# Chunk attention and a leaky-ReLU MLP in one Trainium2 kernel: weights of one more group turned by TensorE, and another order on SyncE's queue

## The chip, the cores and the metric

The kernel runs on one core of one Trainium2 chip. The metric is the device time of the program on that core in microseconds (us); given times are medians of several runs. All inputs are float32 in device memory, and the result is written there in float32.

## The reference

Attention runs inside chunks of 64 tokens only (batch 8, 8 heads, 576 tokens, head size 64); its result, with the heads side by side, is the input of an MLP of 4608 tokens, 512 wide with 2048 hidden units.

```python
q_c = q.reshape(B, H, nc, chunk, D)          # chunk = 64, nc = 9; k_c and v_c alike
scores = scale * np.matmul(q_c, k_c.transpose(0, 1, 2, 4, 3))
scores = scores - np.max(scores, axis=-1, keepdims=True)
attn = np.exp(scores)
attn = attn / (np.sum(attn, axis=-1, keepdims=True) + 1e-09)
out = np.matmul(attn, v_c)
...
x = np.ascontiguousarray(attn_out.transpose(0, 2, 1, 3)).reshape(B * S, H * D)
h = x @ w_in
g = np.maximum(0.01 * h, h)
return g @ w_out
```

## The kernel before

**Attention by groups.** The 4608 tokens are 36 groups of 128 tokens, each two chunks of 64, all 8 heads. For a group u:

- GpSimd issues the loads of q and k (line 79), which convert to float16; each has 8 buffers.
- q and k are transposed: groups 0 to 9 on TensorE (lines 388 and 393), with a copy out of the bank behind it; from group 10 on by a DMA that SyncE issues (line 409 for q into QT, line 412 for k into KT, 4 buffers each). This is called a *turn* of q or k. GpSimd copies QT into QZ (line 418).
- TensorE makes the scores Sp (line 425). VectorE takes the maximum (435) and subtracts it (439), ScalarE takes the exponential (445), VectorE sums it and inverts the sum (451 to 455), and GpSimd, VectorE for some groups, multiplies the two into the attention weights en (461).
- The weights are transposed into et, which has 4 buffers. For groups 0 to 7, and for those listed in BY_PE (line 42), this is done by four transposes on TensorE (469) and a copy on ScalarE (100) or VectorE (102), called e and d2. For the rest it is a DMA on SyncE's queue (480), called d.
- TensorE multiplies them with the values (491, into xp), and ScalarE copies xp to xT, the input of the MLP (504).

**The MLP by blocks.** Four blocks of 128 tokens (0 to 3) come first, and then eight of 512 (4 to 11). The first layer is plain for blocks 0 to 5 (169, with ScalarE's leaky ReLU at 180); from block 6 on it is a fast product in the manner of Strassen and Winograd (307), with sums on VectorE (216, 219) and copies on ScalarE (183). The second layer is plain for blocks 0 to 3 (194), and fast from block 4 on (355): VectorE forms sums S of pieces of gT (216, 219), TensorE multiplies, and ScalarE and VectorE (219) write the results into osb, which has 3 buffers. SyncE stores osb (line 213 for plain blocks, 367 for fast ones). A fast block has two halves, and each half two sides, so that it is stored in several pieces.

**What sets the order.** Nothing is scheduled while the program is built. It makes a list of steps, such as "scores of group 22" or "turn of k of group 22", and run() emits them in the order of the list ORDER (line 643 on). An entry holds the number of the step, a fill, and the bank of TensorE's accumulator memory or the buffer that the step takes. Each engine's instructions stand in the order in which they are emitted, and each engine works through its own queue in that order: an instruction that waits holds up all that stands behind it on its engine. SyncE's queue holds the turns and the stores together; GpSimd's holds the loads, the copies into QZ and the multiplications of line 461. ON (line 615) names the engine of the steps that have a choice.

A fill such as (39, 7) means that ahead of the step TensorE multiplies ones into bank 7, 39 units of 128 columns (line 510); nobody reads the result. All fills stand in the first 34 us.

```python
def stage_c(u, e):                  # "d2": bank -> et, engine e
def stage_d(u):                     # "d": en -> et by SyncE's DMA
if u < UE or u in BY_PE:            # e and d2, else d
```

Of the kernel before, what the change touches and what calls it, by code (L numbers as in the profile page):

```python
# [16 lines left out]
def kernel(  # L17
# [24 lines left out]
    BY_PE = [8, 9, 18]  # L42
# [567 lines left out]
    def arrive_v(b, c0, c1, after=(), **kw):  # L610
# [6 lines left out]
        ('zv', 0, 2): 'dve', ('zq', 2): 'dve', ('zv', 1, 2): 'act', ('zv', 1, 3): 'act', ('p', 0, 0): 'dve', ('p', 0, 1): 'dve', ('p', 1, 1): 'act',  # L617
        ('p', 1, 0): 'dve', ('zq', 3): 'pool', ('n', 0): 'dve', ('p', 2, 0): 'act', ('p', 2, 1): 'act', ('d2', 0): 'dve', ('v_p', 0, 0): 'act', ('n', 1): 'dve',
        ('v_p', 1, 1): 'act', ('v_p', 2, 1): 'act', ('v_p', 3, 0): 'pool', ('v_p', 0, 1): 'act', ('v_p', 1, 0): 'dve', ('v_p', 3, 1): 'pool',
        ('v_p', 4, 0): 'act', ('v_p', 5, 1): 'act', ('v_p', 2, 0): 'pool', ('d2', 1): 'dve', ('v_p', 4, 1): 'dve', ('v_p', 5, 0): 'dve', ('p', 3, 0): 'dve',  # L620
        ('p', 3, 1): 'dve', ('zv', 2, 1): 'pool', ('n', 2): 'dve', ('d2', 2): 'act', ('zv', 2, 0): 'pool', ('zv', 3, 1): 'act', ('zv', 2, 2): 'pool',
        ('zv', 3, 3): 'act', ('zv', 2, 3): 'pool', ('v_p', 7, 1): 'dve', ('v_p', 6, 1): 'act', ('v_p', 6, 0): 'act', ('p', 4, 1): 'act', ('p', 4, 0): 'dve',
        ('n', 3): 'dve', ('d2', 3): 'dve', ('zv', 3, 2): 'act', ('p', 5, 0): 'act', ('p', 5, 1): 'act', ('v_p', 7, 0): 'pool', ('zv', 3, 0): 'act',
        ('p', 6, 0): 'dve', ('p', 6, 1): 'dve', ('v_p', 8, 0): 'dve', ('v_p', 8, 1): 'dve', ('n', 4): 'dve', ('p', 7, 1): 'dve', ('p', 7, 0): 'dve',
# [525 lines left out]
```

## Time and profile before

| what | value |
|---|---|
| median of 3 runs | 276.37 us (275.36, 276.37, 276.54) |
| profiled execution | 278.43 us |
| its span (first to last instruction on the engines) | 276.7 us |
| granted TensorE clock over the span | 1.0 |
| DMA traffic | 38.64 MB, mean 140 GB/s |

The profile is of one execution. A row of the timeline holds the start, the busy time, the engine, the source line, the operation with its output and its inputs, the shapes, and the number of instructions in the row; in brackets stands the idle time of the engine ahead of the row and what ended it. A row of the list of waits holds the engine and the operation that waited, what released it, the sum, the count and the longest. Rows without a start hold a DMA and its time from issue to landing. SPq and POOLq are the queues of DMAs that SyncE and GpSimd issue: there a row's time is that of the issue. The rows themselves stand with the steps of the prediction that use them.

GpSimd's loads (line 79) and SyncE's turns and stores use the same 16 DMA engines. By slices of 6.9 us, these are busy over 90% from the start to 173 us, as row DMA of the page shows (tenths of busy time):

```profile
DMA  9999999999999999999999999999953050040016
```

### The profile page before, as it was taken

The page shows a single profiled execution, that of the slowest core. Times are in us where ns is not written, and L with a number is a line of the kernel's source. Part 1 is how long each engine was busy: PE and PEld are TensorE (multiplying, and loading weights), DVE is VectorE, ACT ScalarE, POOL GpSimd, SP SyncE. Part 2 cuts the span into 40 slices and gives each one's busy share as a digit, 9 for nine tenths or more (in the row PEclk, how much of TensorE's full clock was granted, in tenths as well). Part 3 has the DMA queues.
Part 4 walks back from the last instruction along what each step waited for, and adds up shares of the span by engine and source line. Part 5 has one row for each costly group of instructions (what it writes and reads, how often), then busy time and mean ns, then how long its engine had stood idle before and what let it go on. Part 6 is the DMA issues. An engine that isn't in the chain of part 4 may idle for free.

```text
span 276.7 us, 7688 instructions
## 1 busy us (share of the span) xinstructions
PE 266.4 (96%) x3116; PEld 231.0 (84%) x3116; DVE 209.7 (76%) x376; ACT 196.5 (71%) x370; POOL 159.7 (58%) x199
## 2 busy tenths in 40 slices
PE   7999999999998999999799999999999999999995
PEld 3568678789897899999699898979999899888884
DVE  5896286869888798899788997868998873825462
ACT  6488955767764835899698549889687897467821
POOL 8999784695996996928927798635653020000000
PEclk9999999999999999999999999999999999999999
DMA  9999999999999999999999999999953050040016
GB/s 135 156 191 185 181 173 176 141 167 209 121 117 153 169 179 163 169 168 191 124 136 189 130 167 183 143 173 143 220 140 40 2 178 14 0 154 0 28 51 229
DMA packets 163635, 38.64 MB, mean 140 GB/s; under 512 B 154640, under 2 KB 159248, under 8 KB 163600
## 3 DMA queue, kind: packets, MB, share of 16 engines
q0 software_dynamic: 114384, 18.09, 101.3%
q1 hardware_dynamic: 48176, 19.80, 41.6%
q8 instruction: 24, 0.39, 0.6%
q10 hardware_dynamic: 1040, 0.26, 0.4%
q14 instruction: 11, 0.09, 0.1%
HBM read 36.70 MB, written 9.44 MB: 167 GB/s over the span
## 4 chain that ended last, share of the span: by engine, by line
PE 74%; DMA 10%; POOL 7%; DVE 4%; issue 2%; ACT 2%; POOLq 0%; DVEq 0%
PE oA L355 17%; PE hA L307 14%; PE hT L169 9%; PE oC L355 9%; PE hC L307 7%; PE oP L194 5%; DMA et<-en 5%; PE oB L355 4%; PE hB L307 4%; DMA KT<-k_in 3%; DMA q_in<-in_q_dram 3%; PE xp L491 2%; PE Sp L425 2%; POOL q_in L79 2%; POOL en L461 2%
## 5 line engine op out<-in xcount | busy, mean ns | idle before, releaser
L355 PEld LDWEIGHTS <-gT 128*128 128x128 f16 x640 | 61.3, 98 | 6.7
L461 POOL TENSOR_TENSOR en<-ex,zi 128x512 f16<-128x512 f16 x23 | 26.5, 1152 | 47.3 <-DVE zi L455 17.6
L219 DVE TENSOR_TENSOR tmp<-hC,tmp 128x512 f32<-128x512 f32 x48 | 32.1, 683 | 19.9 <-PE hC L307 18.1
L169 PE MATMUL hT<-xT,w_inT 128*128 128x128 f16 (+1 forms) x512 | 46.0, 246 | 1.0 <-ACT xT L504 0.9
L169 PEld LDWEIGHTS <-w_inT 128*128 128x128 f16 x512 | 39.4, 98 | 4.8 <-issue 1.3
L307 PEld LDWEIGHTS <-VF 128*128 128x128 f16 x512 | 39.4, 98 | 2.8
L418 POOL COPY QZ<-QT 64x512 f16<-64x512 f16 x52 | 34.8, 669 | 4.0 <-DMA QT<-q_in 1.8
L79 POOL DMA_DIRECT2D q_in<-in_q_dram x39 | 33.6, 864 | 4.6 <-DMA w_outT<-in_moe_w_out_dram 2.5
L79 POOL DMA_DIRECT2D k_in<-in_k_dram x39 | 33.5, 861 | 2.2 <-DVE gT L216 1.1
L183 ACT ACTIVATE tmp<-hA 128x512 f32<-128x512 f32 x48 | 27.7, 598 | 8.9 <-PE hA L307 8.3
L180 ACT ACTIVATE gT<-hT 128x512 f16<-128x512 f32 x48 | 26.6, 599 | 8.9 <-PE hT L169 8.8
L355 PE MATMUL oA<-WF,gT 128*128 128x256 f16 x256 | 32.5, 273 | 0.0
L307 PEld LDWEIGHTS <-w_inT 128*128 128x128 f16 x384 | 30.2, 98 | 2.2
L435 DVE TENSOR_REDUCE mx<-Sp 128x8 f32<-128x512 f32 x36 | 24.5, 682 | 8.4 <-PE Sp L425 8.3
L180 ACT ACTIVATE gT<-tmp 128x512 f16<-128x512 f32 x48 | 29.6, 629 | 1.4 <-DVE tmp L219 1.2
L445 ACT ACTIVATE ex<-sh 128x512 f16<-128x512 f32 x36 | 22.7, 630 | 10.3 <-DVE sh L439 9.3
L451 DVE TENSOR_REDUCE z<-ex 128x8 f32<-128x512 f16 x36 | 24.4, 677 | 5.8 <-ACT ex L445 5.7
L504 ACT ACTIVATE xT<-xp 128x512 f16<-128x512 f32 x36 | 21.2, 599 | 10.1 <-PE xp L491 10.0
L307 PE MATMUL hA<-XF,VF 128*128 128x128 f16 (+1 forms) x256 | 27.5, 246 | 0.0
L355 PEld LDWEIGHTS <-S 128*128 128x128 f16 x256 | 24.5, 98 | 2.7
L439 DVE TENSOR_TENSOR sh<-Sp,mx 128x512 f32<-128x512 f32 x36 | 24.4, 683 | 0.5
L183 ACT ACTIVATE hB<-hA 128x512 f32<-128x512 f32 x24 | 13.9, 588 | 12.1 <-PE hA L307 11.9
(77 smaller groups left out, 493.6 us busy)
## 6 DMA issues: line engine op xcount, KB each, us to landing
out_dram<-osb SPq DMA_DIRECT2D x14, 512.0 KB, 3.8
VB<-in_v_dram POOLq DMA_DIRECT2D x14, 288.0 KB, 7.9
q_in<-in_q_dram POOLq DMA_DIRECT2D x31, 128.0 KB, 7.2
k_in<-in_k_dram POOLq DMA_DIRECT2D x31, 128.0 KB, 6.8
w_inT<-in_moe_w_in_dram POOLq DMA_DIRECT2D x8, 256.0 KB, 7.6
w_outT<-in_moe_w_out_dram POOLq DMA_DIRECT2D x4, 512.0 KB, 9.4
out_dram<-osb SPq DMA_DIRECT2D x6, 256.0 KB, 4.2
v_t<-in_v_dram POOLq DMA_DIRECT2D x4, 128.0 KB, 7.2
```

The lines of the kernel that those rows point to most:

```text
L79: nc.gpsimd.dma_start(out=t[a - u * G:z - u * G], in_=src[b, :, r:r + z - a, :].rearrange("h p d -> p h d"))
L169: nc.tensor.matmul(out=hT[:, i, :], lhsT=w_inT[:, t, fc * 128:(fc + 1) * 128], rhs=xT[:, t, r0 % RING:r0 % RING + tb], start=(i == 0 and t ...
L180: nc.scalar.activation(out=to, in_=of, func=AFT.Prelu, bias=0.0, scale=1.0, alpha=0.01)
L183: nc.scalar.activation(out=to, in_=of, func=AFT.Copy, bias=0.0, scale=1.0)
L219: (nc.vector if e == "dve" else nc.gpsimd).tensor_tensor(out=to, in0=a, in1=b, op=ALU.add)
L307: nc.tensor.matmul(out=PA[key][:, c, :], lhsT=w[:, t, fc * 128:(fc + 1) * 128], rhs=x[:, t, :], start=(m in (1, 5) and c == 0 and t == 0), ...
L355: nc.tensor.matmul(out=to, lhsT=lhs[:, fc, p * 128:(p + 1) * 128], rhs=rhs[:, fc, :], start=(fresh and fc == 0), stop=(fc == HB - 1), skip ...
L418: nc.gpsimd.tensor_copy(out=QZ[u % NQZ][part, :, :, s, :], in_=QT[u][part].rearrange("p i (e t) -> p i e t", e=2))
L435: nc.vector.tensor_reduce(out=MX[u], in_=SP[u], axis=AXL.X, op=ALU.max)
L439: nc.vector.tensor_tensor(out=SH[u], in0=SP.pop(u), in1=MX.pop(u).unsqueeze(2).to_broadcast((128, 8, CH)), op=ALU.subtract)
L451: nc.vector.tensor_reduce(out=z, in_=E[u], axis=AXL.X, op=ALU.add)
L461: eng.tensor_tensor(out=E[u], in0=ex, in1=ZI.pop(u).unsqueeze(2).to_broadcast((128, 8, CH)), op=ALU.mult)
```

## The change

Group 11 is added to BY_PE. Its weights are transposed on TensorE, and copied by VectorE, where SyncE's DMA did it. The list has one step more by this (e and d2 in place of d), so that the numbers in ORDER behind it shift by one, and both tables are written anew.

```diff
-    BY_PE = [8, 9, 18]
+    BY_PE = [8, 9, 11, 18]
...
     ON = {
...
+        ('vf', 1): 'dve', ('n', 11): 'pool', ('d2', 11): 'dve', ('vf', 2): 'dve', ('n', 12): 'pool', ('sf', 4, 2): 'dve', ('n', 13): 'pool', ('vf', 3): 'dve',
...
     ORDER = [
...
-        (115, (9, 1), 3), (113, 0), (88, 0, 4), (13, 0), (116, 0), (89, 0), (144, (5, 1), 5), (117, 0, 6), (18, 0), (145, 0), (90, 0), (118, 0), (23, 0),
```

What the two tables hold differs in these places only:

- **Fills.** The steps keep their places, the numbers change. Ahead of the transposes of q and k of groups 1 to 3, as before: 39, 14, 9, 5 and 67 units, together 134; now 39, 0, 9, 19 and 90, together 157. Around the scores and weights of groups 1 and 2, before 16, 6, 13, 4 and 2 units; now 19, 0, 17 and 4, with 3 ahead of a first-layer block.
- **TensorE.** The second first-layer block of block 1 stands ahead of the transposes of group 2's weights (469), and the values product of group 2 (491) behind a block more. Group 9's weights are transposed one step earlier, ahead of the values product of group 8, and its own values product comes three steps earlier, ahead of the scores of group 11 and a second-layer block. Group 11's transposes stand behind the scores of group 13, and its values product comes one block earlier.
- **ScalarE.** Two copies move, both of group 9. **VectorE.** One copy is added, et of group 11. **GpSimd.** The order is the same.
- **SyncE.** From group 10 on the turns and the stores stand in another order. The last two stores are exchanged.

Banks and buffers have other numbers in many entries; what they hold is the same.

On ScalarE, around 71 us (the evictions gT<-hT are those of block 4's first layer, the two copies et<-tpe and xT<-xp that are moved are those of group 9):

```order
 L100 ACTIVATE et<-tpe 128x512
-L180 ACTIVATE gT<-hT 128x2x256 x4
-L504 ACTIVATE xT<-xp 128x4x128
-L183 ACTIVATE tmp<-oA 128x512
-L100 ACTIVATE et<-tpe 128x512
-L504 ACTIVATE xT<-xp 128x4x128
+L180 ACTIVATE gT<-hT 128x2x256 x3
+L100 ACTIVATE et<-tpe 128x512
+L180 ACTIVATE gT<-hT 128x2x256
+L504 ACTIVATE xT<-xp 128x4x128 x2
+L183 ACTIVATE tmp<-oA 128x512
```

The copy of group 9's weights has moved ahead of an eviction, and its xT ahead of an eviction of an output block.

On SyncE, from the turn of group 17's weights on (some 117 to 135 us). Before, the rows are: weights of group 17, k of 21, store of block 4, q of 22, q of 23, weights of 19, store of block 5's first part, k of 22, weights of 20.

```order
L480 DMA_TRANSPOSE et_2287<-en_2274 128x4x128
L412 DMA_TRANSPOSE KT_2312<-k_in_1877 128x4x128
L367 DMA out_0_dram<-osb_1927 128x2x512
L409 DMA_TRANSPOSE QT_2359<-q_in_1924 128x4x128
L409 DMA_TRANSPOSE QT_2390<-q_in_1819 128x4x128
L480 DMA_TRANSPOSE et_2465<-en_2437 128x4x128
L367 DMA out_0_dram<-osb_2001 128x2x512
L412 DMA_TRANSPOSE KT_2538<-k_in_1976 128x4x128
L480 DMA_TRANSPOSE et_2585<-en_2560 128x4x128
```

Of the change: weights of group 17, q of 22, store of block 4, k of 22, store of block 5's second part, q of 23, weights of 19, weights of 20.

```order
L480 DMA_TRANSPOSE et_2297<-en_2284 128x4x128
L409 DMA_TRANSPOSE QT_2322<-q_in_1900 128x4x128
L367 DMA out_0_dram<-osb_1934 128x2x512
L412 DMA_TRANSPOSE KT_2369<-k_in_1959 128x4x128
L367 DMA out_0_dram<-osb_2333 128x2x512
L409 DMA_TRANSPOSE QT_2420<-q_in_1808 128x4x128
L480 DMA_TRANSPOSE et_2476<-en_2448 128x4x128
L480 DMA_TRANSPOSE et_2593<-en_2568 128x4x128
```

The turn of k of group 22 now stands ahead of group 19's weights, with the store of block 5's second part behind it, which was issued near 148 us before; the store of the first part is gone from here. That one now comes ten rows further on, behind turns of groups 23 to 26 and the weights of group 21:

```order
L412 DMA_TRANSPOSE KT_2621<-k_in_1686 128x4x128
L412 DMA_TRANSPOSE KT_2660<-k_in_2257 128x4x128
L409 DMA_TRANSPOSE QT_2695<-q_in_2501 128x4x128
L409 DMA_TRANSPOSE QT_2744<-q_in_2233 128x4x128
L412 DMA_TRANSPOSE KT_2873<-k_in_2716 128x4x128
L409 DMA_TRANSPOSE QT_2910<-q_in_2623 128x4x128
L480 DMA_TRANSPOSE et_2939<-en_2852 128x4x128
L367 DMA out_0_dram<-osb_1997 128x2x512
```

The fifth row is the turn of k of group 25, which waits for its load, and the last the store of the first part.

On SyncE, some 174 to 190 us. Before: weights of groups 27 and 28, k of 31, store of a part of block 6, k of 32, weights of 29, q of 32.

```order
L480 DMA_TRANSPOSE et_3606<-en_3580 128x4x128
L480 DMA_TRANSPOSE et_3646<-en_3624 128x4x128
L412 DMA_TRANSPOSE KT_3675<-k_in_3285 128x4x128
L367 DMA out_0_dram<-osb_3113 128x2x512
L412 DMA_TRANSPOSE KT_3709<-k_in_3537 128x4x128
L480 DMA_TRANSPOSE et_3735<-en_3713 128x4x128
L409 DMA_TRANSPOSE QT_3764<-q_in_3270 128x4x128
```

Of the change: the store of the part of block 6, k of 31, weights of 27, q of 32, k of 32, weights of 28, k of 33, weights of 29.

```order
L367 DMA out_0_dram<-osb_3123 128x2x512
L412 DMA_TRANSPOSE KT_3546<-k_in_3296 128x4x128
L480 DMA_TRANSPOSE et_3618<-en_3591 128x4x128
L409 DMA_TRANSPOSE QT_3634<-q_in_3280 128x4x128
L412 DMA_TRANSPOSE KT_3660<-k_in_3532 128x4x128
L480 DMA_TRANSPOSE et_3689<-en_3637 128x4x128
L412 DMA_TRANSPOSE KT_3721<-k_in_3476 128x4x128
L480 DMA_TRANSPOSE et_3747<-en_3725 128x4x128
```

The weights of group 28 have moved behind the turn of k of group 32, and those of 29 behind that of 33.

More of the change, by code (lines that the diff above doesn't have):

```diff
@@ L616 @@
         ('zq', 0): 'dve', ('zq', 1): 'dve', ('zv', 0, 3): 'dve', ('zv', 0, 0): 'dve', ('zv', 1, 1): 'act', ('zv', 0, 1): 'dve', ('zv', 1, 0): 'act',
-        ('zv', 0, 2): 'dve', ('zq', 2): 'dve', ('zv', 1, 2): 'act', ('zv', 1, 3): 'act', ('p', 0, 0): 'dve', ('p', 0, 1): 'dve', ('p', 1, 1): 'act',
-        ('p', 1, 0): 'dve', ('zq', 3): 'pool', ('n', 0): 'dve', ('p', 2, 0): 'act', ('p', 2, 1): 'act', ('d2', 0): 'dve', ('v_p', 0, 0): 'act', ('n', 1): 'dve',
-        ('v_p', 1, 1): 'act', ('v_p', 2, 1): 'act', ('v_p', 3, 0): 'pool', ('v_p', 0, 1): 'act', ('v_p', 1, 0): 'dve', ('v_p', 3, 1): 'pool',
@@ L620 @@
[L620 to L623, printed above, removed]
+        ('zv', 0, 2): 'dve', ('zq', 2): 'dve', ('zv', 1, 2): 'act', ('zv', 1, 3): 'act', ('p', 0, 0): 'dve', ('p', 1, 1): 'act', ('p', 0, 1): 'dve',
@@ new lines @@
+        ('p', 1, 0): 'dve', ('zq', 3): 'pool', ('n', 0): 'dve', ('p', 2, 0): 'act', ('d2', 0): 'dve', ('n', 1): 'dve', ('p', 2, 1): 'act', ('v_p', 0, 0): 'act',
+        ('v_p', 1, 1): 'act', ('v_p', 2, 1): 'act', ('v_p', 3, 0): 'pool', ('v_p', 1, 0): 'dve', ('v_p', 0, 1): 'act', ('v_p', 3, 1): 'pool',
+        ('v_p', 4, 0): 'act', ('v_p', 2, 0): 'pool', ('d2', 1): 'dve', ('v_p', 5, 1): 'act', ('v_p', 4, 1): 'dve', ('v_p', 5, 0): 'dve', ('p', 3, 0): 'dve',
+        ('p', 3, 1): 'dve', ('zv', 2, 1): 'pool', ('n', 2): 'dve', ('zv', 2, 0): 'pool', ('zv', 2, 2): 'pool', ('d2', 2): 'act', ('zv', 2, 3): 'pool',
@@ L624 @@
+        ('zv', 3, 1): 'act', ('zv', 3, 3): 'act', ('v_p', 7, 1): 'dve', ('v_p', 6, 1): 'act', ('v_p', 6, 0): 'act', ('p', 4, 0): 'dve', ('n', 3): 'dve',
+        ('p', 4, 1): 'act', ('d2', 3): 'dve', ('v_p', 7, 0): 'pool', ('zv', 3, 2): 'act', ('p', 5, 0): 'act', ('p', 5, 1): 'act', ('zv', 3, 0): 'act',
         ('p', 6, 0): 'dve', ('p', 6, 1): 'dve', ('v_p', 8, 0): 'dve', ('v_p', 8, 1): 'dve', ('n', 4): 'dve', ('p', 7, 1): 'dve', ('p', 7, 0): 'dve',
         ('d2', 4): 'act', ('n', 5): 'dve', ('d2', 5): 'dve', ('wf', 0): 'dve', ('p', 8, 1): 'act', ('wf', 1): 'dve', ('p', 9, 1): 'act', ('wf', 2): 'dve',
[16 rows of a table removed]
[16 rows of a table added]
```

236 rows, old and new, of tables (ON, ORDER) are left out of this document.

## The prediction, made before the changed kernel ran

> **What bounds the kernel now.** I read the page, then TensorE's rows in the list of waits, then the timeline around each wait, then the chain.
>
> ```profile
> PE 266.4 (96%) x3116; PEld 231.0 (84%) x3116; DVE 209.7 (76%) x376; ACT 196.5 (71%) x370; POOL 159.7 (58%) x199
> PE Sp L425 <- DMA KT<-k_in: 2.0, 1, 2.0
> PE hT L169 <- ACT xT L504: 0.9, 2, 0.7
> PE xp L491 <- DMA et<-en: 0.9, 2, 0.5
> ```
>
> TensorE is idle for some 10 us of 276.7. What it waits for, apart from the start, are single late inputs. In order of time:
>
> ```profile
> 9.73 3.78 PE L510 MATMUL idle<-XF 128*128 128x512 f16 x17
> 13.76 0.62 PE L388 MATMUL qp<-ident,q_in 128*128 128x128 f16 x8 [0.25 <-DMA q_in<-in_q_dram]
> 22.56 0.40 PE L469 MATMUL tpe<-ident,en 128*128 128x128 f16 x4 [0.50 <-DVE en L461]
> 74.95 0.81 PE L169 MATMUL hT<-xT,w_inT 128*128 128x256 f16 x6 [0.69 <-ACT xT L504]
> 88.55 0.39 PE L491 MATMUL xp<-et,VB 128*128 128x64 f16 x8 [0.51 <-DMA et<-en]
> 89.62 0.60 PE L169 MATMUL hT<-xT,w_inT 128*128 128x256 f16 x4 [0.22 <-ACT xT L504]
> 134.90 0.39 PE L425 MATMUL Sp<-KT,QZ 128*128 128x64 f16 x8 [1.99 <-DMA KT<-k_in]
> 185.07 0.39 PE L491 MATMUL xp<-et,VB 128*128 128x64 f16 x8 [0.39 <-DMA et<-en]
> ```
>
> The reader is to see the wait in the brackets; each also costs some 0.15 us, because the weight load behind it starts late. But TensorE does not lead everywhere: the chain runs over GpSimd from 67 to 81 us, with hardly a gap, and TensorE catches up with it.
>
> ```profile
> 67.00 1.04 POOL en L461
> 80.27 1.03 POOL en L461
> ```
>
> The profiled execution took 278.43 us, 1.7 more than its span and 2.1 more than the median of 276.37. The sum below is a difference, made on its rows and put on the median.
>
> **The front: more fill.** Ahead of the transposes of q of group 3 (13.76) the fill grows from 14+9+5+67 = 95 to 9+19+90 = 118 units of 128 columns. The 67 units took 3.78 us, 0.056 each, so 23 more are 1.3 us. Their cover is the 0.25 us for which TensorE waited for q, so these transposes come about 1.0 late. Everything up to the weights of group 2 hangs on them, and the transposes of those weights, at 22.56, now also stand behind one more first-layer block; they start about 1.1 later. What they release is ScalarE's queue:
>
> ```profile
> 22.99 0.60 ACT L100 ACTIVATE et<-tpe 128x512 f16<-128x512 f16 x1 [0.29 <-PE tpe L469]
> 33.91 0.60 ACT L504 ACTIVATE xT<-xp 128x512 f16<-128x512 f32 x1
> 34.72 1.06 PE L169 MATMUL hT<-xT,w_inT 128*128 128x128 f16 x16
> ```
>
> Between the first two rows ScalarE has no wait of 0.15 us, so its delay arrives whole at xT of group 3, which TensorE reads at 34.72 at once. The waits at 22.56 and 24 go away on TensorE, and come back as waits for ScalarE. **+1.1** (ends +0.2, if the q loads land a microsecond later than here and hide the fill, and +1.3).
>
> **The moves at 71 and 88.** Group 9's transposes, its values product and, on ScalarE, its two copies come earlier: the product passes a score step and an output block of 0.87, together 1.1 us, more than the wait at 74.95. **-0.8.** Group 11's weights no longer go through SP: the waits at 88.55 and 89.62 go, 0.73 with some 0.3 of weight loads, for four transposes of 0.23. The added copy of 0.4 on VectorE lies beside TensorE's blocks; without that cover it would cost its 0.4. **-0.8.**
>
> **GpSimd stays late.** It follows the scores of groups 8 and 9, which follow the front, so it keeps the front's +1.1 while TensorE has won 1.6.
>
> ```profile
> 92.49 1.06 POOL L461 TENSOR_TENSOR en<-ex,zi 128x512 f16<-128x512 f16 x1
> 93.58 0.63 ACT L445 ACTIVATE ex<-sh 128x512 f16<-128x512 f32 x1
> 94.60 2.05 ACT L180 ACTIVATE gT<-hT 128x512 f16<-128x512 f32 x4
> ```
>
> ScalarE's exp at 93.58 starts as GpSimd's multiply ends (93.55), and the evictions queue behind it. The first, done at 95.2, frees a bank for a block that TensorE began at 95.73. It is now done at 96.3, TensorE is there at 95.2. **+1.0** (ends 0, if the front costs nothing, and 1.2). Up to here +0.5.
>
> **SP between 117 and 150.** This is the core of the change.
>
> ```profile
> 120.22 0.65 SPq L367 DMA_DIRECT2D out_dram<-osb  x1
> 121.01 3.34 SPq L409 DMA_TRANSPOSE QT<-q_in  x2
> 124.88 1.19 SPq L480 DMA_TRANSPOSE et<-en  x1
> 126.52 0.38 SPq L367 DMA_DIRECT2D out_dram<-osb  x1
> 127.07 2.20 SPq L412 DMA_TRANSPOSE KT<-k_in  x1
> ```
>
> The turn of k of group 22 (127.07) stood behind the store of block 5; now it issues some 4 us sooner. The wait at 134.90 goes with its weight load: **-2.1**. But the weights of group 19 (124.88) are now behind that turn and the other store, less one turn: about 1.6 later, 126.5. There they meet loads:
>
> ```profile
> 126.31 0.88 POOL L79 DMA_DIRECT2D k_in<-in_k_dram  x1
> et<-en SPq DMA_TRANSPOSE x1, 2.6
> out_dram<-osb SPq DMA_DIRECT2D x1, 512.0 KB, 6.4
> KT<-k_in SPq DMA_TRANSPOSE x1, 7.7
> 131.62 0.40 PE L491 MATMUL xp<-et,VB 128*128 128x64 f16 x8
> ```
>
> The three middle rows are the landing times of what SP issued at 124.88, 126.52 and 127.07: 2.6 before the load, 6.4 and 7.7 after it. Group 19 is needed at 131.62, now 132.1. It lands between 129.1 (2.6) and 134.2 (7.7); with 6.4, the nearest, at 132.9. **+1.2** with the weight load (ends 0 and 2.3). [...]
>
> The store of block 5 goes the other way, behind the turn of k of group 25, whose input loads late:
>
> ```profile
> k_in<-in_k_dram POOLq DMA_DIRECT2D x1, 128.0 KB, 10.0
> out_dram<-osb SPq DMA_DIRECT2D x1, 512.0 KB, 3.6
> 152.99 0.68 DVE L219 TENSOR_TENSOR osb<-oC,tmp 128x512 f32<-128x512 f32 x1
> 157.29 1.22 DVE L216 TENSOR_TENSOR S<-S,gT 128x2048 f16<-128x2048 f16 x1
> 159.69 0.49 PE L355 MATMUL oA<-WF,S 128*128 128x256 f16 x3
> ```
>
> The load was issued at 133.2 and took 10.0; with +0.5 it lands at 143.7. Three turns of 1.3 follow, so the store issues at 147.6 instead of 126.5. It lands at 151.2 by the store issued at 148.45 (3.6), or 154.0 by its own 6.4. VectorE's sum at 152.99 writes the buffer that it frees, and is due at 152.6 less what has been won; behind it in VectorE's queue is S, which ends at 158.5 with 1.2 us of slack to 159.69. If group 19 cost nothing, the sum is due at 151.4, waits 2.6, and TensorE loses 1.4; else 0 to 0.4. **+0.3** (ends 0 and 1.4).
>
> **SP between 174 and 190.** The weights of groups 28 and 29 now stand behind turns of k:
>
> ```profile
> k_in<-in_k_dram POOLq DMA_DIRECT2D x1, 128.0 KB, 9.0
> 183.91 1.50 SPq L412 DMA_TRANSPOSE KT<-k_in  x1
> et<-en SPq DMA_TRANSPOSE x1, 4.8
> 192.52 0.40 PE L491 MATMUL xp<-et,VB 128*128 128x64 f16 x8
> ```
>
> The load at 174.7 lands at 183.7. Group 32's turn takes 1.3, group 28's 1.3, another turn of k 1.5 (183.91), and group 29 issues at 187.8; with the 4.8 of group 28 before (180.6) it lands at 192.6, against 192.52 less what was won. **+0.6** (ends 0 and 1.2). The wait at 185.07 follows GpSimd and stays. The stores at the end are swapped in pairs that wait for the same blocks: 0.
>
> **Sum:** 1.1 - 0.8 - 0.8 + 1.0 - 2.1 + 1.2 + 0.3 + 0.6 = +0.5: 278.9 for a profiled execution, 276.9 for the median.
>
> **The rivals.** (a) *The queue holds*: landings stay below some 5.5 us, groups 19 and 29 and the store are in time, and only front and GpSimd cost: 1.1 - 1.6 + 1.0 - 2.1 = -1.6, **274.8**. For it speaks that 2.6 and 3.6 occur in the same stretches. Against: the 6.4 and 7.7 beside them. (b) *The wait changes place*, and grows: group 19 lands as the turn of 127.07 did, 7.7 after its issue. It decides from about 5.6 us and takes back more than the 2.1 at 7.7. Then 2.3 for group 19, 0.5 for the store, 1.2 for 28 and 29: 0.5 - 2.1 + 4.0 = +2.4, **278.8**. For it: GpSimd's loads surround this place in both kernels. Against: SP may be held less than I reckon, and then the turn slips in ahead of the load.
>
> **How the numbers follow.** A measurement of this kernel can tell about 0.5% (1.4 us) from no change. The forecast, +0.5, has 0.42; (a) has 0.24; (b) has 0.34, since two of its three pieces need only one late load each. The range reaches to both rivals with little beyond, 274.6 to 279.4; the forecast's own is 275.0 to 277.7. Hence faster 0.24, same 0.42, slower 0.34.
>
> **What would show it.** Right: q of group 3 transposed near 14.8 and no wait for a q load there; no wait at group 9, 11 and 22's places; a new wait for ScalarE near 35 and 96; group 19's values product, or the block behind S near 159, waiting. Wrong: the long fill ends in a wait for q again (the front costs nothing); GpSimd's multiply near 92 not later than before; group 19's turn landing in 3 us; or a new wait of over a microsecond at a place not named here.

## The result and the profile after

| | before | changed |
|---|---|---|
| median | 275.93 us (275.36 to 276.54, 4 runs) | 279.68 us (278.21 to 283.01, 4 runs) |
| ratio | 1 | 1.0119, 95% interval 1.0087 to 1.0151 |
| profiled execution, its span | 278.43, 276.7 | 283.01, 281.2 |

The changed kernel is slower by 1.2%, some 3.3 us. Medians here count all executions, and ratios leave out those that are over 1.5% above the fastest of their kernel, among them the profiled one of the changed kernel, so that a ratio says less than the medians (here 1.36%) where a kernel's executions lie far apart.

TensorE's rows of the list of waits of the changed kernel (sum in us, count, longest; the row of the start, its second, is left out):

```profile
PE xp L491 <- DMA k_in<-in_k_dram: 2.9, 1, 2.9
...
PE xp L491 <- ACT ex L445: 1.3, 1, 1.3
PE kp L393 <- DMA k_in<-in_k_dram: 1.1, 1, 1.1
PE hT L169 <- ACT xT L504: 1.0, 2, 0.6
PE xp L491 <- DMA et<-en: 0.3, 1, 0.3
```

The waits of before for KT (group 22) and for group 11's weights are gone, as forecast, and so is the one for q in the front. In their place stand a wait of 1.15 us for k in the front, one of 1.28 near 84 at group 10's values product, and one of 2.93:

```profile
84.61 0.41 PE L491 MATMUL xp<-et,VB 128*128 128x64 f16 x8 [1.28 <-ACT ex L445]
```

TensorE's timeline around the longest:

```profile
187.00 0.39 PE L491 MATMUL xp<-et,VB 128*128 128x64 f16 x8 [2.93 <-DMA k_in<-in_k_dram]
187.23 1.04 PE L355 MATMUL oA<-w_outT,gT 128*128 128x256 f16 x8
188.10 1.76 PE L307 MATMUL hA<-xT,w_inT 128*128 128x256 f16 x8
189.66 2.89 PE L355 MATMUL oB<-w_outT,gT 128*128 128x256 f16 x16
192.38 1.04 PE L307 MATMUL hA<-XF,VF 128*128 128x256 f16 x8
...
194.15 0.39 PE L491 MATMUL xp<-et,VB 128*128 128x64 f16 x8 [0.29 <-DMA et<-en]
```

The row at 187.00 is the values product of group 27, the one at 194.15 that of group 28. Behind the wait the rows are slow: eight matmuls of 256 columns take 1.76 us at 188.10 and 1.04 at 192.38. The table by stretches shows why (start and end, length, busy time and count of TensorE, then the granted clock, the DMA share and GB/s):

```profile
186.00:188.00 2.00, 1.00 (x16) 1.00 0.96 75
188.00:190.00 2.00, 2.00 (x13) 0.56 1.94 138
190.00:192.00 2.00, 2.00 (x13) 0.59 2.32 151
192.00:194.00 2.00, 1.86 (x18) 1.00 1.58 174
```

The clock was lowered to half for some 3.4 us, which cost about 1.7 more, an estimate (half of 3.4). What group 27 waited for is seen in SyncE's timeline, and in the landing times of what GpSimd issued at 174.29 (the load of k of group 32) and SyncE at 178.64 (the turn of group 27's weights):

```profile
174.49 0.53 SPq L367 DMA_DIRECT2D out_dram<-osb  x1
175.19 1.32 SPq L412 DMA_TRANSPOSE KT<-k_in  x1
178.64 1.22 SPq L480 DMA_TRANSPOSE et<-en  x1
179.95 1.24 SPq L409 DMA_TRANSPOSE QT<-q_in  x1
187.62 1.19 SPq L412 DMA_TRANSPOSE KT<-k_in  x1
188.90 1.37 SPq L480 DMA_TRANSPOSE et<-en  x1
```

```profile
k_in<-in_k_dram POOLq DMA_DIRECT2D x1, 128.0 KB, 13.3
et<-en SPq DMA_TRANSPOSE x1, 8.2
```

Before, that turn stood ahead of the store and of the turn of k; it is the first of the two in the first row here, and landed after 6.4 us:

```profile
178.50 3.38 SPq L480 DMA_TRANSPOSE et<-en  x2
181.98 1.21 SPq L412 DMA_TRANSPOSE KT<-k_in  x1
183.28 0.53 SPq L367 DMA_DIRECT2D out_dram<-osb  x1
et<-en SPq DMA_TRANSPOSE x1, 6.4
```

So the turn of group 27's weights was issued when it was before (178.64, 178.50), but a store of 512 KB and a turn of k now stand ahead of it, and it landed after 8.2 us, at 186.86, 0.14 before the product began. (The wait's row names a load of k instead; it was issued at 171.15 and landed at 186.15, so the turn came last.) Behind it the turn of k of group 32 waited for its load until 187.62, and held back the weights of 28.

### The profile page after: what moved, and what is told of

It is laid out like the page before. It is cut to its first block, busy times and chain, and to the rows that moved or that the text cites. A ratio compares the mean times of both kernels' runs of the same rounds, so it can differ in the third digit from the quotient of the medians.

```text
span 281.2 us, 7702 instructions
## 1 busy us (share of the span) xinstructions
PE 268.9 (96%) x3125; PEld 232.8 (83%) x3125; DVE 209.5 (74%) x377; ACT 196.3 (70%) x370; POOL 161.1 (57%) x199
## 4 chain that ended last, share of the span: by engine, by line
PE 69%; DMA 12%; DVE 6%; ACT 6%; POOL 5%; issue 1%; POOLq 0%; DVEq 0%; ACTq 0%
PE oA L355 16%; PE hA L307 12%; PE hT L169 11%; PE oC L355 8%; DMA k_in<-in_k_dram 8%; PE hC L307 6%; PE oP L194 3%; PE oB L355 3%; PE hB L307 3%; PE xp L491 2%; DMA KT<-k_in 2%; PE Sp L425 2%; DMA et<-en 2%; ACT gT L180 2%; DVE sh L439 1%
## 5 line engine op out<-in xcount | busy, mean ns | idle before, releaser
L418 POOL COPY QZ<-QT 64x512 f16<-64x512 f16 x52 | 35.8, 689 | 3.8 <-DMA QT<-q_in 1.7
```

Of the source, the lines that this page charges most:

```text
L418: nc.gpsimd.tensor_copy(out=QZ[u % NQZ][part, :, :, s, :], in_=QT[u][part].rearrange("p i (e t) -> p i e t", e=2))
```

## The experiments

Two theories. **A**: the new order of SyncE's queue from 172 us on makes the loss. **B**: the loads land late there in any order, and TensorE, which the change brings ahead, has to wait for them. A rival to both is that the single profile misled, and that the front makes the loss.

**The change again.** No edit.

> The changed kernel once more, for a second profile. If the order of SyncE's queue makes the loss: 1.012 of before again (277.5 to 280 us), with group 10's values product waiting about 1.3 us near 84 and group 27's 1.5 to 3 us near 185. If the one profiled execution only had late loads: those two waits are under 0.6 us, and what is slower stands in the front, or is spread.

Median 280.43 us of 12 (276.70 to 283.91), ratio 1.0113 (1.0070 to 1.0156). Before, beside it: 275.5 of 23 (274.17 to 278.07). The profile again has its waits at groups 27 and 28, and apart from the start and 1.1 us for xT they are all that TensorE waits for:

```profile
184.43 0.39 PE L491 MATMUL xp<-et,VB 128*128 128x64 f16 x8 [2.67 <-DMA et<-en]
192.30 0.39 PE L491 MATMUL xp<-et,VB 128*128 128x64 f16 x8 [2.68 <-DMA et<-en]
```

The 1.28 us for group 10 near 84 did not come back; that was one execution's. Executions of the changed kernel now lie 7 us apart, those of before 4.

**Two transfers back behind group 27.**

```diff
 L480 DMA_TRANSPOSE et<-en 128x4x128        (26)
-L367 DMA out_dram<-osb 128x2x512
-L412 DMA_TRANSPOSE KT<-k_in 128x4x128      (31)
 L480 DMA_TRANSPOSE et<-en 128x4x128        (27)
+L367 DMA out_dram<-osb 128x2x512
+L412 DMA_TRANSPOSE KT<-k_in 128x4x128      (31)
```

> The change, with the store of a part of block 6 and the turn of k of group 31 put back behind the turn of group 27's weights. Theory (those two transfers delay that turn): its landing falls from 8.2 to about 6.5 us, group 27's values product waits under 0.6 us, and the time is 1.5 to 2.5 us under the change's. Rival 1 (the turn is late because loads are late): same time as the change. Rival 2 (the wait moves to groups 28 and 29, whose turns stay behind the turn of k of group 32): the wait at 27 goes, one of about 2 us shows at 28 or 29, and the time falls by under 0.7 us.

281.76 us of 6, ratio 1.0172 (1.0117 to 1.0227): the time did not fall. In its profile the turn of 27 landed after 4.5 us and group 27 did not wait; groups 28 and 29 did, 0.84 and 2.26 us. These are rival 2's waits, so that the turn of 27 isn't the only cause. That the edit took group 27's wait away isn't shown by this one execution: its load of k of 32 came early (7.8 us), and the turn of 27 landed after 4.1 and 4.5 us in two executions with the change's own order (below).

**Group 10's turn put back ahead.** The turn of group 10's weights ahead of a store and of the turn of q of 14.

> The change, with the turn of group 10's weights put back ahead of the turn of q of group 14 and of a store. Theory (these two hold it back): it issues near 72.5 in place of 74.8, lands near 80, the 1.3 us wait near 84 goes, and the time falls by 1.0 to 1.5 us. Rival (TensorE then only comes earlier to ScalarE's or GpSimd's chain near 90 to 97): the wait goes, another of about 1 us comes before 100 us, and the time is the change's within 0.4 us.

282.75 us of 6, ratio 1.0202 (1.0145 to 1.0259). No gain: its wait had not been there in the second profile either. Groups 27 and 28 waited 2.77 and 1.82 us.

**The front as before.**

```diff
-(112, 0, 2) ... (144, (19, 1), 5) ... (170, (90, 3), 7) ... (146, (19, 6), 2), (123, 0, 3)
+(112, (14, 2), 2) ... (144, (5, 1), 5) ... (170, (67, 3), 7) ... (146, (16, 6), 2), (123, (6, 3), 3)
-(96, (17, 0), 4) ... (98, (3, 3), 1) ... (154, 0, 5)
+(96, (13, 0), 4) ... (98, 0, 1) ... (154, (2, 5), 5)
```

with the first-layer blocks (129) behind the transposes (152), and (102) behind the values product (154).

> The change, with the fills and the order of TensorE up to 26 us as before. By the prediction the front costs 1.1 us: xT of group 3 is read near 35 in place of 36.4, and the time falls by about 1.1 us. Rival (later waits, for group 10 near 84 and group 27 near 185, take up what the front gives): the first-layer blocks of block 3 start 1.1 us earlier and the time is the change's within 0.4 us.

279.01 us of 12 (275.03 to 285.69), ratio 1.0064 (1.0022 to 1.0106): about 0.5%, or 1.4 us, less than the change, with intervals that overlap. In this profile block 3 starts at 34.25 (36.39 and 35.32 with the change). It also fell on an execution in which the loads came early: the load of k of 32 took 7.3 us in place of 13.3 and 14.0, the turn of 27 landed after 4.1, and groups 27 to 29 waited less than 0.1 us although the queue's order was the change's. So the order makes the kernel depend on how fast the loads are.

**SyncE's order from 172 us on, both ways.** In the change it is put back to that of before; in the kernel before, it alone is put in. The edit in the kernel before, from the weights of group 26 on:

```diff
-L480 DMA_TRANSPOSE et<-en 128x4x128 x3     (26, 27, 28)
-L412 DMA_TRANSPOSE KT<-k_in 128x4x128      (31)
+L480 DMA_TRANSPOSE et<-en 128x4x128        (26)
 L367 DMA out_dram<-osb 128x2x512
-L412 DMA_TRANSPOSE KT<-k_in 128x4x128      (32)
-L480 DMA_TRANSPOSE et<-en 128x4x128        (29)
+L412 DMA_TRANSPOSE KT<-k_in 128x4x128      (31)
+L480 DMA_TRANSPOSE et<-en 128x4x128        (27)
+L409 DMA_TRANSPOSE QT<-q_in 128x4x128      (32)
+L412 DMA_TRANSPOSE KT<-k_in 128x4x128      (32)
+L480 DMA_TRANSPOSE et<-en 128x4x128        (28)
+L412 DMA_TRANSPOSE KT<-k_in 128x4x128      (33)
+L480 DMA_TRANSPOSE et<-en 128x4x128        (29)
...
```

> The change, with SyncE's queue from the turn of group 26's weights to that of group 31's as before: the weights of 27 and 28 ahead of the turn of k of group 31, of the store and of the turns of k of 32 and 33. Theory A (this order makes the loss): groups 27 to 29 wait under 1 us together, the clock is not lowered behind them, and the time is 4 to 6 us under the change's (276 to 274 us, at or below before). Theory B (the loads land late there whatever the order, and TensorE, which is ahead by some 2.9 us at 134 us, has to wait for them): groups 27 to 29 still wait 2 us or more together, and the time falls by under 2 us.

> The kernel before, with SyncE's queue from the turn of group 26's weights to that of group 31's in the order of the change, nothing else. Theory A: groups 27 and 28 wait 2 to 5 us together, in some executions with a lowered clock behind it, and the time is 1.01 to 1.02 of before. Theory B: TensorE is not ahead here, the loads have landed when they are needed, and the time is within 0.4% of before.

The change with the old order: 276.67 us of 12, ratio 1.0025 (0.9998 to 1.0053). The kernel before with the new order: 279.39 of 6, ratio **1.0150** (1.0101 to 1.0200). The order alone, put into a kernel with none of the other edits, makes a loss as large as the whole change's. TensorE's waits for weights in the kernel before with the new order:

```profile
184.12 0.39 PE L491 MATMUL xp<-et,VB 128*128 128x64 f16 x8 [1.81 <-DMA et<-en]
190.07 0.39 PE L491 MATMUL xp<-et,VB 128*128 128x64 f16 x8 [0.75 <-DMA et<-en]
193.53 0.41 PE L491 MATMUL xp<-et,VB 128*128 128x64 f16 x8 [0.89 <-DMA et<-en]
```

They are groups 27, 28 and 29. In the change with the old order only this is left, and the turn of 27 landed after 2.4 us:

```profile
191.66 0.41 PE L491 MATMUL xp<-et,VB 128*128 128x64 f16 x8 [0.22 <-DMA et<-en]
```

A holds, and B does not: TensorE was not ahead in the kernel before. But A says 4 to 6 us under the change, down to the time of before or less. By the ratios it was 2.6 (0.94%), by the medians of all executions, each against the kernel before that ran beside it, 4.0, and it did not come under before. What is left of the change does not gain.

**The two halves of the order**, each put into the kernel before alone. First, the store and the turn of k of 31 ahead of the weights of 27, with 28 still ahead of the turn of k of 32; then the weights of 28 and 29 behind the turns of k of 32 and 33, with 27 left where it was.

```diff
-L480 DMA_TRANSPOSE et<-en 128x4x128 x3     (26, 27, 28)
+L480 DMA_TRANSPOSE et<-en 128x4x128        (26)
+L367 DMA out_dram<-osb 128x2x512
 L412 DMA_TRANSPOSE KT<-k_in 128x4x128      (31)
-L367 DMA out_dram<-osb 128x2x512
+L480 DMA_TRANSPOSE et<-en 128x4x128 x2     (27, 28)
```

```diff
-L480 DMA_TRANSPOSE et<-en 128x4x128 x3     (26, 27, 28)
+L480 DMA_TRANSPOSE et<-en 128x4x128 x2     (26, 27)
...
 L412 DMA_TRANSPOSE KT<-k_in 128x4x128      (32)
+L480 DMA_TRANSPOSE et<-en 128x4x128        (28)
+L412 DMA_TRANSPOSE KT<-k_in 128x4x128      (33)
 L480 DMA_TRANSPOSE et<-en 128x4x128        (29)
```

> The kernel before, with the store of a part of block 6 and the turn of k of group 31 ahead of the turn of group 27's weights; the weights of 28 stay ahead of the turn of k of group 32. If transfers that are issued ahead hold back the turn of group 27: it lands some 2 us later than where it stands alone, group 27 waits 1.5 to 2 us, and the time is 1.005 to 1.008 of before. If only the turns that wait for loads matter (next run): within 0.3% of before.

> The kernel before, with the weights of group 28 behind the turn of k of group 32 and those of 29 behind that of group 33; the weights of 27 stay where they were. If turns that wait for loads hold back what stands behind them: no wait of over 0.5 us at group 27, 1 to 3 us at groups 28 and 29 together, and the time is 1.004 to 1.010 of before. If the loss is all in the turn of group 27: within 0.3% of before. By both causes together the two runs add up to the 1.015 of the whole order.

277.48 us of 12, ratio 1.0059 (1.0031 to 1.0086), and 278.49 of 6, ratio 1.0105 (1.0069 to 1.0141), the first as expected, the second just above the expected 1.010. Together 1.64%, against 1.50% for the whole order. Each half has its own wait, group 27's in the first and group 29's in the second:

```profile
183.20 0.39 PE L491 MATMUL xp<-et,VB 128*128 128x64 f16 x8 [1.66 <-DMA et<-en]
```

```profile
192.54 0.41 PE L491 MATMUL xp<-et,VB 128*128 128x64 f16 x8 [1.29 <-DMA et<-en]
```

The landing time of the turn of 27 in the first, and in the second:

```profile
et<-en SPq DMA_TRANSPOSE x1, 7.5
```

```profile
et<-en SPq DMA_TRANSPOSE x1, 4.8
```

**The gain that was expected near 135, alone.** In the kernel before, the turn of k of 22 ahead of the turn of q of 23, the weights of 19 and the store.

```diff
-L409 DMA_TRANSPOSE QT<-q_in 128x4x128 x2   (22, 23)
+L409 DMA_TRANSPOSE QT<-q_in 128x4x128      (22)
+L412 DMA_TRANSPOSE KT<-k_in 128x4x128      (22)
+L409 DMA_TRANSPOSE QT<-q_in 128x4x128      (23)
 L480 DMA_TRANSPOSE et<-en 128x4x128        (19)
 L367 DMA out_dram<-osb 128x2x512
-L412 DMA_TRANSPOSE KT<-k_in 128x4x128      (22)
```

> The kernel before, with the turn of k of group 22 ahead of the turn of q of 23, of the weights of 19 and of the store, nothing else. Theory A: the wait of 2.0 us near 135 goes, group 19's weights land in time, and the time is 1.5 to 2.1 us under before (0.993). Theory B: the wait goes and comes back between 180 and 195 us, since TensorE then is ahead of the loads: within 0.4% of before.

275.44 us of 12, ratio 0.9982 (0.9958 to 1.0007): at most 1.2 us, likely 0.5, as B says, but not for B's reason. Its profile has no wait for KT, and none of over 0.1 us between 180 and 195 either. The gain was not taken back: it was hardly there. In the kernel before with the new order from 172 us on, which is the kernel before up to there, the same wait is

```profile
PE Sp L425 <- DMA KT<-k_in: 0.3, 1, 0.3
```

0.3 again in the first half above, and none in the second. The 2.0 us of the first profile were that execution's, and it was 2.1 over the median.

**What is left of the change.** The change with both the front and the order from 172 us on as before, and then with the turn of group 19's weights also ahead of a store and of the turn of q of 23:

```diff
 L412 DMA_TRANSPOSE KT<-k_in 128x4x128      (22)
+L480 DMA_TRANSPOSE et<-en 128x4x128        (19)
 L367 DMA out_dram<-osb 128x2x512
 L409 DMA_TRANSPOSE QT<-q_in 128x4x128      (23)
-L480 DMA_TRANSPOSE et<-en 128x4x128 x2     (19, 20)
+L480 DMA_TRANSPOSE et<-en 128x4x128        (20)
```

> The change, with the front (fills and TensorE's order up to 26 us) and SyncE's queue from 172 us as before. Theory A: 1 us better than the run with the queue alone, 272 to 274 us, the best of all: 0.985 to 0.993 of before. Theory B: waits at groups 27 to 29 take up both, and the time is that of before within 0.5%.

> The change, with the front and SyncE's queue from 172 us as before, and the turn of group 19's weights ahead of the store of block 5's second part and of the turn of q of group 23. The wait of 0.76 us that stood at group 19 near 132 goes; if nothing later takes it up, the time is 0.5 to 1 us under the run without this move, 0.997 of before; if GpSimd near 95 to 100 and the loads set the pace, it is that run's, 1.000.

275.83 us of 12, ratio 1.0009 (0.9981 to 1.0037), and 275.79 of 12, ratio 1.0009 (0.9988 to 1.0030): the time of before, twice, where A expected 272 to 274 of the first. B expected this time, but by waits at groups 27 to 29, and neither profile has one there of over 0.1 us. Group 19 waited 0.76 us in the first and not in the second, as expected, and it did not show in the time. TensorE's waits in the second, apart from its first 16 us:

```profile
PE hT L169 <- ACT gT L180: 0.8, 1, 0.8
PE Sp L425 <- POOL QZ L418: 0.6, 1, 0.6
```

They stand at 95.2 and 87.9: with the front early again, the 1.6 us that the prediction gives the moves at 71 and 88 end in waits for ScalarE and for GpSimd, 1.3 us of idle time.

**Fill in the wait**, against the lowered clock.

```diff
-(959, 0, 2) ... (1069, 0, 1)
+(959, (24, 2), 2) ... (1069, (24, 1), 1)
+l, r = (ones[:, :128], ones[:, :w]) if n_idle[0] <= 8 else (ident, w_inT[:, 0, :w])
```

> The change, with 24 units of fill (1.35 us, ident and w_in, result unread) ahead of the values products of groups 27 and 28 each, into the bank that the product takes; they run in the wait. If the lowered clock follows from TensorE's idle time there: idle times stay under 2 us, no run has a clock under 0.997, and the time is 0.5 to 1.5 us under the change's on the median, with less spread. If the lowered clock has another cause: as many runs at 0.994 as with the change, and the time is the change's or up to 1.5 us longer, where the loads come in time.

280.44 us of 6, ratio 1.0164 (1.0136 to 1.0192); one execution of six had a mean clock of 0.994, against four of twelve with the change. No gain, and too few to say whether the fill keeps the clock up; its profile fell on an execution with early loads (the turn of 27 landed after 4.5 us), which had no wait there.

## Why the forecast came out as it did

The forecast was 276.9, within 0.5% of before. It came out 1.2% slower, past rival (b)'s 278.8, at the upper end of the range (279.4; the median of the four executions, 279.68, lies 0.3 beyond it). The mechanism was of (b)'s kind, a wait that changes place and grows. But of (b)'s three pieces only groups 28 and 29 came, and the largest, group 27, is not among them. By the prediction's own last sign, a new wait of over a microsecond at a place that it does not name, it was wrong: 2.93 us at group 27 and two shorter ones in the first profile, 2.67 at group 27 in the second. Step by step:

- **Front, +1.1: right.** Block 3's first layer started at 35.2 to 37.7 us in six profiles with the change's front, median 35.7, and at 33.8 to 35.2 in eight with that of before, median 34.4: 1.3. On the time it was 0.5% beside the late queue, and 0.16% without it, where waits for other engines come instead.
- **Moves at 71 and 88, -1.6: right on the spot.** Group 11's weights were not waited for in any profile with the moves; in four of five others they were, 0.4 to 1.3 us. It did not reach the end.
- **GpSimd stays late, +1.0: too large.** Its multiply of 92.49 stood at 94.76 in the first profile of the change, and at 90.70 in the second. With the change's front the wait at 95 to 97 was 0 to 0.45 us. With the front as before, where TensorE arrives sooner, it and a wait for QZ beside it came to 0.9 and 1.3 us in two profiles and to nothing in a third.
- **Turn of k of 22, -2.1: mis-sized.** The row was right, and it was one execution's. Measured: -0.5 us alone, with an interval up to +0.2. That the profiled execution was 2.1 over the median stood in the prediction, but its rows were then used as if they were the median's.
- **Group 19, +1.2, and the store, +0.3.** The turn landed 6.1 us after its issue (6.4 was taken), and the store was issued at 148.16 and took 3.5 (147.6 and 3.6 were taken). Both came just in time behind the late front: no wait.
- **SP between 174 and 190, +0.6: this step failed.** The text ahead of the prediction has the DMA engines busy to 173 us; its row shows 29 of 40 slices, so to 200, and the loads were running here too. The prediction held that "the wait at 185.07 follows GpSimd and stays". The time of issue did follow GpSimd; the landing did not stay, because a store and a turn had been put ahead of it. With them it landed in 7.5 to 8.2 us in five profiles, and in 4.1 and 4.5 in two with early loads; without them in 2.4 to 6.4 in seven. That is 0.59%, 1.6 us. The other half, groups 28 and 29 behind the turns of k of 32 and 33, was seen and was mis-sized: 1.05%, 2.9 us, where 0.6 was taken. Its own profile shows 1.29 us of that, at group 29 and with a load that landed in time; in profiles of the change, where that load took 12.6 to 14.0 us in place of 9.0, group 28 waited up to 2.7. The rest of the 2.9 isn't located.

Put along the runs, the prediction's terms and what was measured in their place are these (us):

| part of the change | terms | measured | by |
|---|---|---|---|
| moves, turn of k of 22, group 19, store | -2.2 | +0.2 | 1.0009, the change with the front and the order from 172 us as before |
| front, with GpSimd behind it | +2.1 | +0.4 | 1.0025 less 1.0009 |
| order from 172 us on | +0.6 | +2.6 | 1.0119 less 1.0025 |
| sum | +0.5 | +3.3 | |

The measured parts add up because each is a difference to the next kernel; each is good to about 1 us. By the medians of all executions, with the second measurement of the change, they are +0.1, +0.8 and +4.0. The order put alone into the kernel before gave 4.1, which would leave the rest at -0.8. So two terms were off by over 2 us the same way, the gains up to 135 us and the order from 172 on, and the front's, 1.7 too large, hid a part of it. That the time came out near the range is luck in that measure.

What stays open: why the load of k of group 32 took 7.3 and 7.8 us in two executions with the change's order, and 12.6 to 14.0 in three. The order may be a part of it: with the store ahead, in two more kernels, it took 9.1 and 9.9, and with the store behind 4.8 to 9.0 in seven. These are single executions of different kernels, so this isn't shown.

## What to carry to other kernels

A DMA that TensorE waits for is priced by its landing and not by its issue: a store of 512 KB and a turn put ahead of it cost 1.6 us here, while its own issue did not move. A turn that waits for a load should stand behind the turns whose inputs are ready (the weights of groups 28 and 29 behind such turns cost 1.05%, 2.9 us, here), above all where the load's time varies between executions as here, from 7 to 14 us. A wait that one profile shows is worth only what other profiles of the same kernel show of it, all the more if that profile is longer than the median by as much as the wait.

## What the runs showed of the hardware that was not expected

The granted clock fell to half for 3.41 us in four of the profiles: 1.1 to 1.3 us after the end of waits of 2.93 us (first profile of the change), 2.77 (group 10's turn put back ahead) and 2.68 (second profile of the change), and at the end of one of 2.26 (two transfers back behind group 27); by an estimate, half of 3.41, this cost 1.7 us each time. It did not fall after another of 2.67, in the second profile of the change too, nor after those of 1.99 (before), 1.82 (group 10's turn put back ahead) and 1.81 (the new order in the kernel before). So the length of the wait alone does not tell it: 2.26 had a fall, and 2.67 had none.

In the 3.41 us ahead of each of the four falls, TensorE was idle for 2.1 to 2.3 us. In the second profile of the change, these are the 3.41 us ahead of the fall behind the wait of 2.68, and those of the fall itself, with length, busy time and clock as above:

```profile
190.19:193.60 3.41, 1.30 (x18) 1.00 1.25 173
193.60:197.01 3.41, 3.41 (x24) 0.50 1.21 126
```

That does not tell it either: the wait of 2.67 left more idle time in a stretch of this length, and no fall came. What decides it isn't shown.
